# Attention's results and half of its queries turned by transposing transfers instead of TensorE

## The chip, the cores and the metric

The kernel runs on one core of one Trainium2 chip. The metric is the time of one execution on the device, in microseconds (us); of several executions the median is given.

A core has five engines with a queue of instructions each: TensorE (PE) multiplies matrices and writes to PSUM only; VectorE (DVE), ScalarE (ACT) and GpSimd (POOL) work on elements; SyncE (SP) here only issues transfers. Transfers (DMAs) are issued from SP's queue or POOL's and move data between main memory and SBUF, or within SBUF. Each queue works in its order, and an instruction that has to wait holds up those behind it.

## The reference, cut to what matters

Two layers in a row. The first is attention in which every block of 96 tokens looks at one block of mixed keys and values; the mixing matrix comes from five Sinkhorn steps:

```python
# B, H, S, D = 4, 8, 768, 64; 8 blocks of 96 tokens
k_sorted = einsum('bhij,bhjcd->bhicd', P, k_b)
v_sorted = einsum('bhij,bhjcd->bhicd', P, v_b)
scores = scale * matmul(q_b, k_sb.T)          # within a block: 96 x 96
attn = exp(scores - max) ; attn /= sum
attn_out = matmul(attn, v_sb)
x = attn_out.transpose(0, 2, 1, 3).reshape(B * S, H * D)   # 3072 x 512
```

The second is a mixture of eight experts, all of them applied to all 3072 tokens and weighted by a table P that comes from eight Sinkhorn steps over the logits of all tokens:

```python
logits = x @ w_gate                            # 512 x 8
for e in range(8):
    out += P[:, e:e+1] * (maximum(x @ w1[e], 0) @ w2[e])
```

The inputs are float32; the kernel multiplies in bfloat16 and accumulates in float32.

## The kernel before, in words

**Layout.** A batch's keys, values and queries come into SBUF (`load_batch`, L67, issued by POOL, which converts them to bfloat16) with the 768 tokens spread over 128 partitions, six tokens to a partition. A token is thus named by a partition c and a place kk from 0 to 5. The attention matmuls need the head's 64 channels on the partitions, and the expert layer needs x with its 512 channels on the partitions (`xtT`, four groups of 128 channels, one for each pair of heads). So queries are turned before they are used, and results after.

**Steps of attention.** For each batch bb and pair of heads hp there are five steps. Each has a letter in the plans, so "s2" is the scores of pair 2:

- "k", `keys` (L210): twelve matmuls with the mixing matrix that sort and turn the keys at once; VectorE copies them out of PSUM into `kTs`.
- "q", `queries` (L188): the queries are turned on TensorE. In batches 0 and 1 this takes twelve transposes of 64 channels; in batches 2 and 3 POOL first puts a pair's channels side by side (`qr`, L201) and six transposes of 128 channels follow (L205). ScalarE copies the result out of PSUM into `qTs`, and puts the tokens back into their order as it does so (L208).
- "s", `scores` (L231): sixteen matmuls of 96x96 (L239), and exponentials by ScalarE into `atp` (L247).
- "m", `mix` (L250): sixteen matmuls of the exponentials with the sorted values and a column of ones (L257); VectorE divides by the sums (L260, L261) into `og`, which has tokens on its partitions.
- "t", `turn` (L265): eight transposes on TensorE (L268), and a copy out of PSUM into `xtT` (L271).

The values are sorted by `sort_values` (L176): eight matmuls, copies by ScalarE into `vs`, and then `hop` (L169), which moves them within SBUF from the spread layout into blocks of 96 tokens (`vsb`) by eight transfers, one for each block: the even blocks are issued on SP, the odd ones on POOL (L172). A mix reads all eight. `logits` (L276) multiplies `xtT` by the gate's weights (L283).

**Order.** Batch 0 is attended to first, alone. From there to batch 3, attention is woven together with the expert layer's first expert over batches 0 and 1: `first_two` (L465) is a generator of 56 units of TensorE work, 28 for each batch. A hidden unit is four matmuls with w1 (L379) and an output unit four matmuls with w2 (L388). The strings of steps, such as `usual` (L500), are plans: a comma joins steps, and a blank marks a place where units may be put. `run_both` and `weave` (L451) say how many. The hidden units of batch 1 read batch 1's `xtT`, the first of them right after k0 of batch 2. TensorE keeps its written order, and so do the operations under `pin`; elsewhere a scheduler sets the order of an engine's queue and puts in the waits. `sum_x` (L139) is VectorE's preparation of `xtT` for the later experts.

After batch 3, `last_two` (L739) does the first expert for batches 2 and 3, `balance` (L554) the eight Sinkhorn steps, and the other seven experts follow in a scheme that takes seven products where eight would be usual (`hidden`, L595, and `output7`, L673). That part is some four fifths of the run.

## Time and profile before

| | |
|---|---|
| Median of three executions | 680.24 us (679.92 to 681.83) |
| The profiled execution | 679.37 us, of which the span from the first to the last instruction is 677.4 us |
| TensorE busy | 651.2 us, 96% of the span |
| VectorE, ScalarE, POOL busy | 541.6, 298.2, 473.5 us |
| Batch 0, up to its last turn | about the first 31 us |
| Attention of batches 1 to 3 with the first expert | about 31 to 113.5 us |
| First expert on batches 2 and 3, balance, second expert begun | 113.5 to 171 us |
| Experts 1 to 7 | to the end |

How to read it: a line of the timeline gives the start in us from the span's start, the length, the engine, the line of the kernel, what is written and read, and how many alike follow one another; a bracket at the end tells how long the engine was idle before it and what released it. Matmuls are pipelined: a group's length includes some 0.17 us until the last result is out, so the cost of a group on TensorE is read from its start to the start of the next one. For transfers the time from issue to landing is given. "SPq" is the time of an instruction on SP's queue.

### The profile page before, as it was taken

To read this page: it belongs to the slowest core of one execution; us is meant where nothing else is said; L and a number is where in the kernel's file an instruction comes from. 1 tells how busy PE (TensorE), PEld (TensorE's weight loads), DVE (VectorE), ACT (ScalarE), POOL (GpSimd) and SP (SyncE) were. 2 spreads that over 40 slices of the span, in tenths; PEclk is the share of its full clock that TensorE was granted. 3 is DMA by queue.
4 is the path that set the end of the run, shared out by engine and by line. 5 is a ranking of instruction groups with operands and counts; after the bars stand their busy time and mean duration, and the time that the engine had idled before them with its cause. 6 is when DMAs were issued, how large, how long until landed. Compare 5 with 4: busy or idle time off the path is not lost.

```text
span 677.4 us, 13154 instructions
## 1 busy us (share of the span) xinstructions
PE 651.2 (96%) x5043; PEld 434.7 (64%) x5122; DVE 541.6 (80%) x1131; ACT 298.2 (44%) x541; POOL 473.5 (70%) x499
## 2 busy tenths in 40 slices
PE   4899999999999999999999999999999999999996
PEld 2656766554666666666666666666666666666675
DVE  6617768663788889888888889888898888888896
ACT  4575763469533343434333343333433343333430
POOL 4542435007987988898997898689886999646745
PEclk9999999999999999999999999999999999999999
DMA  9898973101240340030303040034003120001223
GB/s 159 143 215 132 160 133 47 19 1 24 40 62 1 63 63 1 1 63 10 55 1 57 7 64 1 2 63 63 1 1 64 19 45 1 0 1 63 94 78 141
DMA packets 32415, 36.57 MB, mean 54 GB/s; under 512 B 2016, under 2 KB 25312, under 8 KB 32352
## 3 DMA queue, kind: packets, MB, share of 16 engines
q0 software_dynamic: 26912, 27.82, 25.9%
q1 hardware_dynamic: 5440, 7.90, 3.6%
q8 instruction: 40, 0.66, 0.4%
q14 instruction: 23, 0.19, 0.1%
HBM read 52.45 MB, written 6.29 MB: 87 GB/s over the span
## 4 chain that ended last, share of the span: by engine, by line
PE 72%; DVE 1%; issue 1%; POOL 1%; ACT 0%; DVEq 0%
PE oacc L688 37%; PE bk L601 34%; PE bk L688 1%; DVE osbl L653 1%; POOL hs L671 1%; DVE hT L637 0%; DVE hT L640 0%; ACT p L621 0%; DVEq L653 0%
## 5 line engine op out<-in xcount | busy, mean ns | idle before, releaser
L653 DVE SCALAR_TENSOR_TENSOR osbl<-oacc,glog,osbl 128x256 f32<-128x256 f32 (+1 forms) x490 | 255.6, 522 | 61.3 <-PE oacc L688 61.2
L671 POOL TENSOR_TENSOR hs<-hT 128x512 bf16<-128x512 bf16 (+2 forms) x105 | 99.5, 961 | 68.4 <-DVE hT L640 68.2
L601 PE MATMUL bk<-xtT,w1e 128*128 128x512 bf16 x475 | 143.5, 379 | 0.9
L688 PEld LDWEIGHTS <-hT 128*128 128x128 bf16 x1008 | 98.6, 98 | 64.5 <-issue 1.3
L688 PEld LDWEIGHTS <-hs 128*128 128x128 bf16 x1008 | 98.5, 98 | 64.6 <-POOL hs L671 1.5
L688 PE MATMUL oacc<-w2e,hT 128*128 128x256 bf16 x796 | 119.6, 273 | 1.0 <-ACT hT L643 0.5
L643 ACT ACTIVATE hT<-bk 128x512 bf16<-128x512 f32 x84 | 50.3, 599 | 158.7 <-PE bk L601 140.9
L671 POOL TENSOR_TENSOR hs<-hT,hs 128x512 bf16<-128x512 bf16 (+2 forms) x105 | 100.0, 959 | 4.9
L671 POOL TENSOR_TENSOR hs<-hs,hT 128x512 bf16<-128x512 bf16 (+2 forms) x105 | 99.9, 959 | 4.2 <-ACT hT L643 0.4
L601 PE MATMUL bk<-xc,wc 128*128 128x512 bf16 x319 | 96.2, 379 | 0.6 <-ACT p L621 0.2
L688 PE MATMUL oacc<-w2e,hs 128*128 128x256 bf16 x612 | 92.0, 273 | 1.6 <-POOL hs L671 0.9
L629 ACT COPY u<-bk 128x512 f32<-128x512 f32 x84 | 49.3, 587 | 95.2 <-PE bk L601 83.6
L601 PEld LDWEIGHTS <-w1e 128*128 128x128 bf16 x672 | 65.7, 98 | 10.5
L637 DVE CUSTOM_DVE_ANT_0 hT<-bk,p 128x512 bf16<-128x512 f32 x84 | 58.1, 692 | 11.8 <-ACT p L634 6.4
L647 DVE SCALAR_TENSOR_TENSOR h<-bk,hT 128x512 bf16<-128x512 f32 x84 | 57.2, 681 | 5.7 <-ACT hT L643 5.7
L634 ACT COPY p<-bk 128x512 f32<-128x512 f32 x84 | 49.4, 588 | 23.5 <-PE bk L601 23.5
L621 ACT COPY p<-bk 128x512 f32<-128x512 f32 x84 | 49.4, 588 | 20.1 <-PE bk L601 20.1
L625 DVE CUSTOM_DVE_ANT_0 hT<-bk,p 128x512 bf16<-128x512 f32 x84 | 57.2, 681 | 1.1 <-ACT hT L381 0.6
L640 DVE CUSTOM_DVE_ANT_0 hT<-bk,u 128x512 bf16<-128x512 f32 x84 | 57.2, 680 | 1.0 <-PE bk L601 1.0
L688 PE MATMUL oacc<-w2s,hs 128*128 128x256 bf16 x364 | 54.8, 273 | 0.3
L601 PEld LDWEIGHTS <-wc 128*128 128x128 bf16 x504 | 49.3, 98 | 8.0 <-issue 0.4
L601 PE MATMUL bk<-xtT,wc 128*128 128x512 bf16 x159 | 48.0, 379 | 0.0
(136 smaller groups left out, 827.9 us busy)
## 6 DMA issues: line engine op xcount, KB each, us to landing
w2e<-in_moe_w_dram POOLq DMA_DIRECT2D x8, 1024.0 KB, 8.8
w1e<-in_moe_w_dram POOLq DMA_DIRECT2D x7, 1024.0 KB, 8.3
out_dram<-osbl SPq DMA_DIRECT2D x23, 256.0 KB, 2.0
kvq<-in_v_dram POOLq DMA_DIRECT2D x3, 768.0 KB, 9.0
kvq<-in_k_dram POOLq DMA_DIRECT2D x3, 768.0 KB, 11.6
vsb<-vs SPq DMA_DIRECT2D x16, 97.5 KB, 4.5
vsb<-vs POOLq DMA_DIRECT2D x16, 97.5 KB, 4.0
kvq<-in_q_dram POOLq DMA_DIRECT2D x4, 384.0 KB, 9.6
```

The source lines that it names most:

```text
L601: hold(nc.tensor.matmul(ps, wa[:, kk, :], xa[:, kk, :], start=(first and kk == 0), stop=(kk == 1), skip_group_check=True))
L621: nc.scalar.copy(p1, u)
L625: nc.vector._custom_dve(TENSOR_ADD_SAT, out=c11, in0=w, in1=p1, s0=TOP, s1=0.0)
L629: nc.scalar.copy(u2, u)
L634: nc.scalar.copy(p5, v)
L637: nc.vector._custom_dve(TENSOR_ADD_SAT, out=c22, in0=u, in1=p5, s0=TOP, s1=0.0)
L640: nc.vector._custom_dve(TENSOR_ADD_SAT, out=c12, in0=v, in1=u2, s0=TOP, s1=0.0)
L643: nc.scalar.activation(out=c21, in_=u, func=AF.Relu)
L647: nc.vector.scalar_tensor_tensor(out=h3[e, p][:, i, :], in0=u, scalar=0.0, in1=c22, op0=ALU.max, op1=ALU.subtract)
L653: nc.vector.scalar_tensor_tensor(out=o, in0=ps, scalar=glog[:, t, e:e + 1], in1=o, op0=ALU.mult, op1=ALU.add)
L671: nc.gpsimd.tensor_tensor(out=c, in0=a, in1=b, op=o)
L688: nc.tensor.matmul(ps, h[:, fb, :], w[:, fb, :], start=(first and fb == 0), stop=(fb == 3), skip_group_check=True)
```

## The change

Three kinds of turns leave TensorE, and what they need is rearranged:

- **Results.** For batches 1 and 2, and for three of the four pairs of batch 3, `turn` issues one transposing transfer on SP that reads `og` (96 tokens by 1024) and writes the pair's part of `xtT` (128 channels by 768 tokens). Batch 0 and the last pair of batch 3 stay on TensorE.
- **Queries of batches 2 and 3.** A new function, `queries_across`, has POOL put all four pairs of a batch side by side (`qr`) and issues one transposing transfer for each on SP, from 128 partitions of 768 into `qTs`. It is called ahead of the batch's value sort. Batch 1's queries stay on TensorE.
- **The tokens' order.** The transfer leaves a batch's queries in the order kk, c where ScalarE's copy had made c, kk of it. The score matmuls of these batches therefore read six runs of 16 tokens, and the exponentials read PSUM across and write in the tokens' order.
- **Buffers.** `og` and `qr` have four buffers instead of two.
- **Plans.** All four query steps of batch 1 now come before its scores; mixes and turns stand together; batch 1's logits come after three places of batch 2, batch 2's after three places of batch 3, and batch 3's near the end; the units of the first expert are dealt out anew, 56 as before. Batch 2's value sort comes after m3 of batch 1 instead of before it.

In SP's queue the order around each seam becomes: the four turns of a batch, the four query transfers of the next batch, and that batch's four transfers of sorted values.

```diff
@@ queries
-        if bb < 2:
-            for kk in range(6):
-                for h in range(2):
-                    pin(nc.tensor.matmul(qps[64 * h:64 * h + 64, kk, :], ...
-        else:
-            qr = sp.tile([128, 6, 2, 64], BF16, name="qr", bufs=2)
-            nc.gpsimd.tensor_copy(
-                qr.rearrange("p kk h d -> p h kk d"),
-                qt[bb][:, 2 * hp:2 * hp + 2].rearrange("p h (kk d) -> p h kk d", d=64))
-            for kk in range(6):
-                pin(nc.tensor.matmul(qps[:, kk, :], qr[:, kk].rearrange("p h d -> p (h d)"),
+        for kk in range(6):
+            for h in range(2):
+                pin(nc.tensor.matmul(qps[64 * h:64 * h + 64, kk, :],
+                                     qt[bb][:, 2 * hp + h, kk * 64:kk * 64 + 64],
                                      Ibig, is_transpose=True, start=True, stop=True))
+    def queries_across(bb):
+        for hp in range(4):
+            qr = sp.tile([128, 6, 2, 64], BF16, name="qr", bufs=4)
+            pin(nc.gpsimd.tensor_copy(
+                qr.rearrange("p kk h d -> p h kk d"),
+                qt[bb][:, 2 * hp:2 * hp + 2].rearrange("p h (kk d) -> p h kk d", d=64)))
+            qT[bb, hp] = sp.tile([128, 6, 128], BF16, name="qTs", bufs=4)
+            pin(nc.sync.dma_start_transpose(
+                out=qT[bb, hp], in_=qr.rearrange("p kk h d -> p (kk h d)")))
@@ scores
-                        qT[bb, hp][r, 16 * i:16 * i + 16].rearrange("p c kk -> p (c kk)"),
+                        (qT[bb, hp][r, :, 16 * i:16 * i + 16] if bb > 1 else
+                         qT[bb, hp][r, 16 * i:16 * i + 16].rearrange("p c kk -> p (c kk)")),
...
+                if bb > 1:
+                    to = to.rearrange("p j (c kk) -> p j c kk", kk=6)
+                    of = of.rearrange("p j (kk c) -> p j c kk", kk=6)
+                nc.scalar.activation(out=to, in_=of, func=AF.Exp, scale=scale)
@@ mix
-            og[bb, hp] = sp.tile([128, NB, 2, 64], BF16, name="og", bufs=2)
+            og[bb, hp] = sp.tile([128, NB, 2, 64], BF16, name="og", bufs=4)
@@ turn
+        if 0 < bb < 3 or bb == 3 and hp < 3:
+            pin(nc.sync.dma_start_transpose(
+                out=xtT[:, hp, bb * S:(bb + 1) * S].rearrange("p (i c) -> p i c", i=NB),
+                in_=og[bb, hp][0:96].rearrange("p i h d -> p (i h d)")))
+            return
@@ the order
-        at1 = attention(1, bank1, "k0 k1 k2 q0 q1 s0 q2 s1 k3 q3 s2 "
-                                  "m0 s3 m1,t0 m2,t1 m3 t2 t3,l0 l3")
-        run_both(at1, (1, 1, 1, 1, 0, 1, 0, 1, 1, 0, 1))
+        at1 = attention(1, bank1, "k0 k1 k2 q0 q1 q2 q3 s0 s1 k3 s2 "
+                                  "m0,t0 s3 m1,t1 m2,t2 m3,t3")
+        run_both(at1, (1, 1, 1, 1, 0, 0, 0, 1, 1, 1, 1))
         load_batch(2, [(x, 0, 8) for x in "vkq"])
         build_r(2, nc.gpsimd, 4)
-        run_both(at1, (1, 1, 1, 1))
+        run_both(at1, (1, 1, 1, 1, 1))
+        queries_across(2)
         run_both(sort_values(2, bank1), (1, 0, 1, 0, 1))
-        run_both(at1, (1, 0, 0, 0))
-        usual = "q0,q1,k0 k1,s0,q2 k2,s1,q3 m0 k3,s2 m1,t0 s3 m2,t1 m3 t2 t3,l0 l3"
+        usual = "k0 k1,s0 k2,s1 m0,t0 k3,s2 m1,t1 s3 m2,t2 m3 t3"
...
+            weave(at1, ex, 3, 3)
+            logits(bb - 1, bank1, (0, 1, 2, 3))
+            weave(at1, ex, 2, 2)
+            if bb == 2:
+                load_batch(3, [(x, 0, 8) for x in "vkq"])
+                build_r(3, nc.gpsimd, 4)
+                weave(at1, ex, 5, 4)
+                queries_across(3)
+                weave(sort_values(3, bank1), ex, 5, 5)
             else:
...
+                weave(at1, ex, 2, 4)
+                logits(3, bank1, (0, 1, 2, 3))
```

More of the change, by code (lines that the diff above doesn't have):

```diff
@@ L191, in queries @@
             qps = bank([128, 6, 128], BF16)
-        if bb < 2:
-            for kk in range(6):
-                for h in range(2):
-                    pin(nc.tensor.matmul(qps[64 * h:64 * h + 64, kk, :],
-                                         qt[bb][:, 2 * hp + h, kk * 64:kk * 64 + 64],
-                                         Ibig, is_transpose=True, start=True, stop=True))
-        else:
-            qr = sp.tile([128, 6, 2, 64], BF16, name="qr", bufs=2)
-            nc.gpsimd.tensor_copy(
-                qr.rearrange("p kk h d -> p h kk d"),
-                qt[bb][:, 2 * hp:2 * hp + 2].rearrange("p h (kk d) -> p h kk d", d=64))
-            for kk in range(6):
-                pin(nc.tensor.matmul(qps[:, kk, :], qr[:, kk].rearrange("p h d -> p (h d)"),
+        for kk in range(6):
+            for h in range(2):
+                pin(nc.tensor.matmul(qps[64 * h:64 * h + 64, kk, :],
+                                     qt[bb][:, 2 * hp + h, kk * 64:kk * 64 + 64],
                                      Ibig, is_transpose=True, start=True, stop=True))
@@ L246, in scores @@
                     new_at(bb, hp, h)
-                nc.scalar.activation(out=at[bb, hp, h][0:96, 4 * b:4 * b + 4],
-                                     in_=sps[h][0:96], func=AF.Exp, scale=scale)
+                to, of = at[bb, hp, h][0:96, 4 * b:4 * b + 4], sps[h][0:96]
+                if bb > 1:
+                    to = to.rearrange("p j (c kk) -> p j c kk", kk=6)
+                    of = of.rearrange("p j (kk c) -> p j c kk", kk=6)
+                nc.scalar.activation(out=to, in_=of, func=AF.Exp, scale=scale)
     def mix(bb, hp, h, bank):
         if h == 0:
-            og[bb, hp] = sp.tile([128, NB, 2, 64], BF16, name="og", bufs=2)
+            og[bb, hp] = sp.tile([128, NB, 2, 64], BF16, name="og", bufs=4)
         for b in range(2):
@@ L334, in wide_mix @@
     def wide_mix(hp, pair, extra):
-        og[0, hp] = sp.tile([128, NB, 2, 64], BF16, name="og", bufs=2)
+        og[0, hp] = sp.tile([128, NB, 2, 64], BF16, name="og", bufs=4)
         for h in range(2):
@@ L363, in step @@
                 turn(bb, hp, bank, nc.vector.tensor_copy)
-            elif what == "l":
-                logits(bb, bank, (0, 1, 2) if hp == 0 else (3,))
             else:
@@ L491 @@
         run_both(sort_values(1, bank1), (1, 1, 1, 1, 0))
-        at1 = attention(1, bank1, "k0 k1 k2 q0 q1 s0 q2 s1 k3 q3 s2 "
-                                  "m0 s3 m1,t0 m2,t1 m3 t2 t3,l0 l3")
-        run_both(at1, (1, 1, 1, 1, 0, 1, 0, 1, 1, 0, 1))
+        at1 = attention(1, bank1, "k0 k1 k2 q0 q1 q2 q3 s0 s1 k3 s2 "
+                                  "m0,t0 s3 m1,t1 m2,t2 m3,t3")
+        run_both(at1, (1, 1, 1, 1, 0, 0, 0, 1, 1, 1, 1))
         load_batch(2, [(x, 0, 8) for x in "vkq"])
         build_r(2, nc.gpsimd, 4)
-        run_both(at1, (1, 1, 1, 1))
+        run_both(at1, (1, 1, 1, 1, 1))
+        queries_across(2)
         run_both(sort_values(2, bank1), (1, 0, 1, 0, 1))
-        run_both(at1, (1, 0, 0, 0))
-        usual = "q0,q1,k0 k1,s0,q2 k2,s1,q3 m0 k3,s2 m1,t0 s3 m2,t1 m3 t2 t3,l0 l3"
-        for bb, ns in ((2, (5, 3, 2, 4)), (3, (5, 4, 0, 5))):
+        usual = "k0 k1,s0 k2,s1 m0,t0 k3,s2 m1,t1 s3 m2,t2 m3 t3"
+        for bb in (2, 3):
             at1 = attention(bb, bank1, usual)
-            weave(at1, ex, 5, ns[0])
-            if bb + 1 < B:
-                load_batch(bb + 1, [(x, 0, 8) for x in "vkq"])
-                build_r(bb + 1, nc.gpsimd, 4)
+            weave(at1, ex, 3, 3)
[7 more added lines that the diff above has]
+                weave(sort_values(3, bank1), ex, 5, 5)
             else:
@@ L509 @@
                 sums = sum_w(1)
-            weave(at1, ex, 3, ns[1])
-            if bb + 1 < B:
-                weave(sort_values(bb + 1, bank1), ex, 5, ns[2])
-            else:
+                weave(at1, ex, 3, 4)
                 for _ in sums:
@@ L518 @@
                     next(x0)
-            weave(at1, ex, 4, ns[3])
-        for _ in ex:
-            pass
+                weave(at1, ex, 2, 4)
+                logits(3, bank1, (0, 1, 2, 3))
+                for _ in ex:
+                    pass
     actx.close()
```

## The prediction

> **What bounds the kernel now.** I read the busy shares first, then the windows by stage, then TensorE's order of work inside the stage that changes, and last the transfers. The page and the windows say that TensorE is the bound nearly everywhere:
>
> ```profile
> PE 651.2 (96%) x5043; PEld 434.7 (64%) x5122; DVE 541.6 (80%) x1131; ACT 298.2 (44%) x541; POOL 473.5 (70%) x499
> ...
> PE 72%; DVE 1%; issue 1%; POOL 1%; ACT 0%; DVEq 0%
> ```
>
> ```profile
> 66.00:114.00 48.00, 46.65 (x682) 32.68 (x685) 35.93 (x111) 28.27 (x64) 24.84 (x29) 1.00 0.65 107
> ```
>
> The second fence is the stage of batches 2 and 3 (columns: stretch, then busy time and count of PE, PEld, DVE, ACT, POOL, then clock, DMA share, GB/s). TensorE is busy 46.65 of 48 us, so work taken from it there shortens the run, unless a wait takes its place. The order of its work around the seam between batches 1 and 2, in the timeline (start, length, work):
>
> ```profile
> 65.46 0.88 PE L257 MATMUL bank<-vsb,atp 96*96 96x65 bf16 x16
> 66.39 0.81 PE L388 MATMUL bank<-w2e,hTs 128*128 128x512 bf16 x3
> 67.04 1.07 PE L268 MATMUL bank<-Ibig,og 96*128 96x96 bf16 x16
> ...
> 68.83 0.30 PE L283 MATMUL bank<-wg,xtT 128*128 128x8 bf16 x6 [0.43 <-DVE xtT L271]
> 69.29 0.30 PE L283 MATMUL bank<-wg,xtT 128*128 128x8 bf16 x6 [0.16 <-DVE xtT L271]
> 69.45 0.83 PE L205 MATMUL bank<-Ibig,qr 128*128 128x128 bf16 x12
> 70.21 0.53 PE L218 MATMUL bank<-R,kvq 128*64 128x128 bf16 x12
> ...
> 72.37 0.51 PE L205 MATMUL bank<-Ibig,qr 128*128 128x128 bf16 x6
> 72.72 0.81 PE L379 MATMUL bank<-xtT,w1e 128*128 128x384 bf16 x4
> ...
> 79.72 0.51 PE L268 MATMUL bank<-Ibig,og 96*128 96x96 bf16 x8
> 80.07 0.82 PE L379 MATMUL bank<-xtT,w1e 128*128 128x384 bf16 x4
> ```
>
> The reader is to take from it what a step costs from its start to the next start: a turn of results (L268) 0.35, a turn of one head pair's queries (L205) 0.35 to 0.38, a feed-forward unit 0.65 (L379) or 0.865 (L388), a key group (L218) 0.46, a mix (L257) 0.70, a score group (L239) 0.49. TensorE waits only where a brace stands. The transfers of the sorted values (L172, issued in three different places) show what SP's queue costs:
>
> ```profile
> L172 SPq DMA_DIRECT2D vsb<-vs x16: 571/624/1167, 17.6 to 90.0; - x16
> ...
> DMA to landing us min/median/max: 2.8/4.1/6.8
> ```
>
> One such transfer of 97.5 KB holds SP's queue 0.57 to 1.17 us and lands 2.8 to 6.8 us after its issue. Asked by window, those at 87 to 91 us took 2.9 to 3.7, those at 65 to 69 us 2.8 to 5.5, and those at 42 to 46 us, with weights and inputs in flight, 5.6 to 6.8.
>
> **What goes.** Eleven turns of results: 11 x 0.345 = 3.8 us of TensorE. Eight turns of queries: 0.76 + 0.35 + 0.33 for batch 2 and 0.76 + 0.35 + 0.34 for batch 3 = 2.9 us. The waits beside them go as well: 0.43 and 0.16 (logits on the copy of the turned results), 0.24 twice (a query turn on ScalarE's copy, at 74.72 and 97.41) = 1.07. Two query turns of batch 1 (q2, q3; 0.46 each) move ahead of the first use of the second weight, where TensorE now waits 1.17 us for a transfer: 0.92 of that is filled. Sum: -8.7 us. The copies out of PSUM that go with them (11 x 0.54 on VectorE, 8 x 0.8 on ScalarE) were off the path, for VectorE is busy 36 and ScalarE 28 of the 48 us; I count nothing for them.
>
> **What is added beside the path.** The exponentials of batches 2 and 3 read PSUM across (32 of 497 ns). The nearest row is ScalarE's own strided copy: 814 ns (L208) against 799 for a plain one (L271) of the same 768 columns, 2%, so 0.3 us on an engine with 20 us to spare: nothing. The score matmuls of these batches (128, pitch 31 ns) read their queries in six runs of 16 instead of one run of 96. No row shows TensorE reading so; from nothing to a doubled pitch, +4.0 us. I take nothing, as the runs are still contiguous, and keep the 4.0 for the range. The larger buffers cost nothing in time. On POOL the eight query copies stay (about 1.07 us each with VectorE busy beside it), but the four of batch 2 now stand in front of POOL's share of the sorted values, and batch 3's loads follow at once: from the landing of batch 2's queries at 62.7 us, 4 x 1.07 + 2.15 gives 69.2 us for those loads, against 72.2 now.
>
> **What is added on SP's queue.** Nineteen transposing transfers of 192 KB. Their price, X us of SP's queue each, is in no row. The nearest is the sorted-value transfer on the same queue. Ends: 0.62, if only the issue counts, and 2.9, if the queue is held until the data has landed. By bytes (1.97 times as many) the plain issue of 0.57 to 1.17 becomes 1.1 to 2.3; I take 1.8. Landing, from issue: 2.9 at least.
>
> What matters is what is queued behind them. In program order SP now does t3 of a batch, the four query turns of the next, and only then its four transfers of the sorted values, which mix 0 of that batch reads. Count both ways from the end of m3's matmuls.
>
> Batch 1 to 2. TensorE's way to m0: four output units (3.46), eight value sorts (1.30), three key groups (1.38), three hidden units (1.95), two score groups (0.98), logits (0.60) = 9.7, and 0.26 more to block 6, the last that SP brings. SP's way: VectorE finishes m3 1.36 us after TensorE (67.70 against 66.34 now), then t3 and four queries, 5 x 1.8 = 9.0, then 2.2 to the fourth issue (65.6 to 67.8 now), then the landing. Batch 3's loads are in flight by then (69.2 us on; the fourth issue stands near 73), so I take the slow end of the neighbouring window, 5.5, not 3.2. Total 18.1, against 9.9: a wait of 8.1 us, in pieces block by block. t3 itself is needed 5.2 us after m3 and lands at 4.3 to 7; q0 is needed at 6.3 and lands at 6.1 or later; both small waits lie inside the 8.1.
>
> Batch 2 to 3. TensorE has two more output units, so 11.4 + 0.26 = 11.7. SP: 1.36 + 9.0 + 2.2 + 3.2 = 15.8 (no load in flight). Wait: 4.1.
>
> The end of batch 3 keeps t3 on TensorE, and t0 to t2 have over 3 us before logits: nothing. From 172 us on the same program runs.
>
> Sum: -8.7 + 8.1 + 4.1 = +3.5 us. The profiled execution took 679.37 us (span 677.4 and 2.0 around it), 0.87 below the median of 680.24. So 682.9 against its own time, 683.7 as a median.
>
> **Where a page of notes bears on it.** The row first: 97.5 KB move between places in SBUF and land in 2.8 us at best. The Trainium skill, "VectorE: DVE Perf Modes", section "The three transpose paths", gives 1,309 ns for one 128x128 block of bf16 by transfer, against 390 on TensorE; by it six blocks in a row would take 7.9 us, and the sum would be that of the block rival below, whose number is worked out there from rows; no row here shows such a transfer. The other rule is a worry of a second kind. The first stage has 128x384 matmuls of 521 ns (L292), against 326 later (L179), though the granted clock reads 1.00 in both. The Trainium skill, "TensorE: Matmul & The Clock Gate", section on rules for kernel authors, says that a gap of over about 3 us brings half speed back; by it the wait of 8.1 us would cost some 2 us more. The trace shows both speeds, but no gap that long in mid-run.
>
> **The rivals.**
>
> *Cheap issue: faster.* If X is 0.62, SP's way for batch 2 is 1.36 + 3.1 + 2.2 + 3.2 to 5.5 = 9.9 to 12.2, a wait of 0 to 2.2. Batch 3 then waits on another chain: its queries land 14.4 us after an issue at 71 (85.4), POOL's four copies end at 89.2 or so, SP's values land at 95, and m0 is due at 89.5: 5.7, or 3.5 if batch 2 has waited. Sum -3.0: 677.2; down to 671.5 if this chain is quicker too. At X = 1.25 the sum is -8.7 + 5.4 + 1.3 = -2.0. The sign turns near X = 1.45. For it: SP has issued in 0.57. Against it: that was half the bytes, and unturned.
>
> *Even: within 0.3%.* X of 1.25 to 1.6, where the waits eat just what was saved: 678.5 to 682.
>
> *Block by block: much slower.* The transfer is worked off in blocks and the queue is held meanwhile; at X = 4 the waits are 19 and 15, TensorE also stands at t3 and q0 inside them, and the sum is +25.5: 705.7. For it: landing took up to 6.8 us for half the bytes. Against: those had eight transfers in flight.
>
> *Shared engines.* The turned transfers collide with batch 3's loads; a longer landing there alone moves the time by 2 to 3 us and is in the forecast.
>
> **How the numbers follow.** A measurement of this kernel tells 0.3% (2 us) from no change. Forecast (X from 1.6 to 2.9, 682 to 695): 0.42. Block by block: 0.09. Even: 0.13. Cheap issue: 0.36. So slower 0.51, same 0.13, faster 0.36. The range goes from 674.5 (cheap issue, half of its lower tail) to 695 (X = 2.9: waits of 13.6 and 9.6, +14), which takes in the 4.0 of the score matmuls at the forecast X. The forecast's own range is 682 to 695.
>
> **What would show it.** Transposing transfers on SP with 1.6 us or more from one issue to the next; TensorE's longest new waits at m0 of batches 2 and 3, released by the sorted-value transfers that SP issued (L172), not at t3's hidden unit or at s0; 136 fewer transposes on TensorE; nothing new after 172 us. Wrong if SP's sorted-value transfers are issued within 8 us of t3's issue, if the score matmuls' pitch rises, or if TensorE waits for POOL's query copies.

## The result: 3.4% slower, outside the range

The changed kernel takes 701.88 us (median of four executions, 700.95 to 710.87), the kernel before 680.74 us beside it: a ratio of 1.034, 95% interval 1.029 to 1.038. The forecast was 683.7 us with a range of 674.5 to 695.0. It had the side right, with a chance of 0.51, and the size wrong by 18 us.

The first profiled execution was the longest of the four, 710.87 us, 9 us above the others. I therefore had the same kernel run once more: 702.99 us in the median, and a profiled execution of 701.98 us with a span of 700.2. Unless it says otherwise, "after" below means this second profile. Line numbers are those of the changed kernel: mixes are L262, scores L240, logits L293, the transfers of the sorted values still L172, the queries' transfers L208, the results' L272.

TensorE's share on the page of the first profile, and its part in the chain that ended last, against 96% and 72% before:

```profile
PE 659.1 (93%) x4986; PEld 433.2 (61%) x4986; DVE 536.4 (76%) x1120; ACT 293.3 (41%) x533; POOL 471.7 (67%) x499
...
PE 69%; DVE 1%; POOL 1%; issue 0%; ACT 0%; DVEq 0%
```

The stage of batches 2 and 3 in the second profile (same columns as before):

```profile
66.00:114.00 48.00, 28.21 (x364) 17.89 (x360) 20.39 (x57) 17.65 (x43) 15.92 (x22) 0.83 1.01 160
```

5122 weight loads have become 4986: the 136 transposes are gone. But in the stage that they left, TensorE is now busy 28 of 48 us instead of 47 (364 matmuls fall into them instead of 682, since the stage lasts longer), and the granted clock is 0.83 on average, where it was 1.00. These are the places where it stands, in the timeline (start, length, work, and in the bracket the idle time before and its releaser):

```profile
80.96 0.37 PE L262 MATMUL bank<-vsb,atp 96*96 96x65 bf16 x2 [8.22 <-DMA vsb<-vs]
...
82.45 0.37 PE L262 MATMUL bank<-vsb,atp 96*96 96x65 bf16 x2 [0.50 <-DMA vsb<-vs]
...
111.54 0.37 PE L262 MATMUL bank<-vsb,atp 96*96 96x65 bf16 x2 [7.12 <-DMA vsb<-vs]
...
112.94 0.30 PE L262 MATMUL bank<-vsb,atp 96*96 96x65 bf16 x2 [1.02 <-DMA vsb<-vs]
...
114.34 1.17 PE L262 MATMUL bank<-vsb,atp 96*96 96x65 bf16 x12 [1.10 <-DMA vsb<-vs]
...
133.58 0.48 PE L293 MATMUL bank<-wg,xtT 128*128 128x8 bf16 x12 [4.92 <-DMA xtT<-og]
```

The first two belong to mix 0 of batch 2, the next three to mix 0 of batch 3, the last to batch 3's logits, which wait for the transfer t2. SP's queue in the same profile (start, time until the last of a group is issued):

```profile
66.25 7.78 SPq L208 DMA_TRANSPOSE qTs<-qr  x4
74.12 3.29 SPq L172 DMA_DIRECT2D vsb<-vs  x4
...
95.69 6.98 SPq L208 DMA_TRANSPOSE qTs<-qr  x4
102.77 3.88 SPq L172 DMA_DIRECT2D vsb<-vs  x4
```

So the sorted values stand behind the four query transfers, as forecast. And this is what one transfer costs (length in ns on the queue, least, median and most; then the time from issue to landing):

```profile
L208 SPq DMA_TRANSPOSE qTs<-qr x8: 1210/1228/3653, 66.2 to 99.7; - x8
...
DMA to landing us min/median/max: 2.7/3.9/10.8
```

The least is what matters first: 1.21 us on the queue (1.37 from one issue to the next) and 2.7 us to land, less than the 1.8 and 2.9 of the forecast. The most is what went wrong: the last of each four held the queue for 3.0 to 3.7 us and landed after 9.6 and 10.8. The results' transfers in the same view; the one that took 9.1 us to land is t2 of batch 3:

```profile
L272 SPq DMA_TRANSPOSE xtT<-og x11: 1212/1256/2279, 56.5 to 124.4; - x11
...
DMA to landing us min/median/max: 2.8/4.0/9.1
```

The granted clock behind the waits (second number from the start of the line: TensorE's busy us; third from the end: the clock):

```profile
77.00:81.00 4.00, 0.04 (x1) 0.04 (x2) 0.00 (x0) 0.00 (x0) 0.00 (x0) 0.51 1.24 208
81.00:84.00 3.00, 1.82 (x17) 1.57 (x18) 0.68 (x4) 0.00 (x0) 0.00 (x0) 0.50 1.29 223
84.00:87.00 3.00, 3.00 (x35) 1.77 (x33) 2.24 (x7) 0.74 (x2) 0.00 (x0) 0.50 1.31 203
...
114.00:118.00 4.00, 3.66 (x40) 2.52 (x42) 2.48 (x9) 0.49 (x1) 3.74 (x4) 0.50 0.02 5
...
133.00:136.00 3.00, 2.42 (x18) 1.15 (x19) 0.38 (x2) 0.00 (x0) 0.00 (x0) 0.50 0.00 0
```

It falls to a half while TensorE stands and stays there for 5 to 6.5 us after work goes on. The three stretches at half clock last 10.24, 10.24 and 6.83 us, which is three, three and two steps of 3.41 us; in every trace of this case the half-speed stretches behind waits last one such step or a whole number of them. What the slow clock takes is the busy time times what the clock lacks of 1: over all stretches 2.6 us behind mix 0 of batch 2, 2.2 behind that of batch 3, 2.5 behind the logits, 7.3 in all.

The account of the second profile against the span before (677.4), beside the terms of the forecast:

| | forecast, us | measured, us |
|---|---|---|
| taken from TensorE, with the waits beside it | -8.7 | -8.7, taken over from the forecast (136 loads fewer; the wait for the second weight 0.25 instead of 1.17); the other rows and the span leave -9.4 for it |
| mix 0 of batch 2 | +8.1 | +9.4 (8.22, 0.50, and 0.33 and 0.34) |
| small waits ahead of it | within the 8.1 | +1.4 (0.78 before s0, 0.34 and 0.29 for t2 and t3 of batch 1) |
| mix 0 of batch 3 | +4.1 | +9.2 (7.12, 1.02, 1.10) |
| logits of batch 3 | 0 | +4.9 |
| slow clock | in words, about 2, not in the sum | +7.3 |
| sum | +3.5 | +23.5, where the span is 22.8 longer |

### The profile page after: what moved, and what is told of

It reads as the page before. It is cut to its first block, busy times and chain, and to the rows that moved or that the text cites. A ratio compares the mean times of both kernels' runs of the same rounds, so it can differ in the third digit from the quotient of the medians.

```text
span 709.1 us, 12989 instructions
## 1 busy us (share of the span) xinstructions
PE 659.1 (93%) x4986; PEld 433.2 (61%) x4986; DVE 536.4 (76%) x1120; ACT 293.3 (41%) x533; POOL 471.7 (67%) x499
## 4 chain that ended last, share of the span: by engine, by line
PE 69%; DVE 1%; POOL 1%; issue 0%; ACT 0%; DVEq 0%
PE oacc L699 35%; PE bk L612 34%; PE bk L699 1%; DVE osbl L664 1%; POOL hs L682 1%; DVE hT L648 0%; DVE hT L651 0%; ACT p L632 0%; DVEq L664 0%
## 5 line engine op out<-in xcount | busy, mean ns | idle before, releaser
L612 PE MATMUL bk<-xtT,w1e 128*128 128x512 bf16 x504 | 149.9, 380 | 0.0
L612 PE MATMUL bk<-xc,wc 128*128 128x512 bf16 x336 | 100.1, 380 | 0.2 <-ACT p L632 0.2
L612 PE MATMUL bk<-xtT,wc 128*128 128x512 bf16 x168 | 50.0, 380 | 0.0
```

The costliest lines, as they stand in the source:

```text
L612: hold(nc.tensor.matmul(ps, wa[:, kk, :], xa[:, kk, :], start=(first and kk == 0), stop=(kk == 1), skip_group_check=True))
```

## The experiments

All runs are compared with the kernel before on the same chip (679.5 to 680.7 us). Two theories stood at the start. *A, collision*: a transposing transfer alone is cheap, but it and whatever POOL has in flight (sorted values, loads of inputs and weights) stretch each other. *B, the queue*: the sorted values come late because of the order on SP alone. The second run of the changed kernel was expected so:

> The changed kernel once more, for a second profile: its first profiled execution took 710.87 us, 9 us over the median of the others, with a wait of 1.92 us for the second weight at 49.9 us and half speed behind it. Expected if that wait is what the first had for itself: no wait over 1 us before 66 us, the waits at mix 0 of 8 to 12 us and 6 to 9 us and the one of about 4 us at the logits of batch 3 as before, and a span of 699 to 702. If the long execution was of the same course: the wait of about 1.9 us again and a span near 709.

It was the first case, 702.99 us (1.036, 1.032 to 1.041), with the course shown above. In the first profile, and in that of the run below with t2 on TensorE, TensorE waited 1.92 and 2.67 us for the second weight from 48 us on, ran at about half speed behind that, and two query transfers of batch 2 took over 14 us to land, where here one took 9.6. Why that weight came late there is open.

### Batch 2: the loads, the queue, or both

Three edits of the changed kernel. The first holds back the loads of batch 3 (and of the first weight) on POOL until the sorted values have landed:

```diff
+        def gate(bb):
+            pin(nc.gpsimd.tensor_copy(
+                held, mkap(vsbt[bb % 2], [[VW, 96], [520, 2]], off=6 * 520 + 519)))
...
+                gate(2)
                 load_batch(3, [(x, 0, 8) for x in "vkq"])
...
+                gate(3)
                 load_w1(1)
```

> The changed kernel, with POOL made to hold back the loads of batch 3 (and of the second half of the first weight) until that batch's sorted values have landed; SP's queue has the same transfers in the same order. Theory A: with nothing large in flight q0 to q3 hold SP 1.2 us each and land in 2.8 to 3.5, the sorted values land in 3 to 4; SP's way is 1.4 + 6.1 + 2.2 + 3.2 = 12.9 against 9.9 of TensorE, so mix 0 of batch 2 waits 2 to 4 us instead of 11.6, mix 0 of batch 3 0 to 2 instead of 8.5, and little slow clock follows; batch 3's loads start some 10 us later and may cost up to 5 at their first use: 682 to 690. Theory B: the order on SP is the same, so the waits at mix 0 stay at 8 to 12 and 6 to 8, and the later loads come on top: 700 to 708.

The second clears SP's queue instead:

```diff
-            eng = nc.gpsimd if i % 2 else nc.sync
+            eng = nc.gpsimd if i % 2 or bb > 1 else nc.sync
```

> The changed kernel, with all eight transfers of the sorted values of batches 2 and 3 issued on POOL, so that nothing stands behind the queries' transfers on SP; the loads of batch 3 follow them on POOL as before. Theory A: the loads still run beside the queries' transfers, so q2 and q3 of batch 2 hold SP 3 to 5 us and land after 9 to 15; the wait moves from mix 0 to scores 2 and 3 and is smaller, 3 to 7 us in batch 2 and 0 to 4 in batch 3, with some slow clock: 686 to 695. Theory B: with the queue free the sorted values land 4 to 6 us after issue, mix 0 of neither batch waits, and no wait takes its place: what is left is the 4.1 at the logits of batch 3 and its clock, 680 to 684.

The third leaves batch 3's loads out:

```diff
-                load_batch(3, [(x, 0, 8) for x in "vkq"])
+                vt[3], kt[3], qt[3] = vt[2], kt[2], qt[2]
```

> The changed kernel without the loads of batch 3 (three of 0.79 MB): batch 3 is computed from batch 2's values, keys and queries, so its part of the output is another. SP's queue has the same transfers in the same order. Theory A (the loads are the larger part of what stretches the transfers): q2 and q3 of batch 2 land after 5 to 7 us instead of 14.5, the sorted values behind them after 3 to 4 instead of 10.5, mix 0 of batch 2 waits 2 to 5 us instead of 11.6, batch 3 waits little, and the granted clock falls less: 682 to 688. Theory B (the order of SP's queue alone): mix 0 of batch 2 still waits 8 us or more, and the time is 695 to 702.

The first took 699.47 us (1.031, 1.028 to 1.034), the second 691.2 (1.017, 1.015 to 1.020), the third 699.93 (1.029, 1.026 to 1.032). The waits of TensorE where the loads are held back:

```profile
78.91 0.37 PE L262 MATMUL bank<-vsb,atp 96*96 96x65 bf16 x2 [4.83 <-DMA vsb<-vs]
...
104.75 0.88 PE L240 MATMUL bank<-qTs,kTs 64*96 64x96 bf16 x16 [5.26 <-DMA qTs<-qr]
...
114.74 0.62 PE L262 MATMUL bank<-vsb,atp 96*96 96x65 bf16 x4 [4.12 <-DMA vsb<-vs]
```

and where there are none:

```profile
76.68 0.37 PE L262 MATMUL bank<-vsb,atp 96*96 96x65 bf16 x2 [4.77 <-DMA vsb<-vs]
...
106.43 0.37 PE L262 MATMUL bank<-vsb,atp 96*96 96x65 bf16 x2 [6.58 <-DMA vsb<-vs]
...
107.88 0.29 PE L262 MATMUL bank<-vsb,atp 96*96 96x65 bf16 x2 [1.09 <-DMA vsb<-vs]
...
128.09 0.48 PE L293 MATMUL bank<-wg,xtT 128*128 128x8 bf16 x12 [4.78 <-DMA xtT<-og]
```

Both ways the first wait at mix 0 of batch 2 falls from 8.2 to 4.8 us: 3.4 of it are the loads. The other 4.8 need no load. With POOL's four transfers of sorted values in flight, the fourth query transfer still held the queue 2.67 us in the run without loads, and 3.56 us where they were held back, and SP's sorted values stood behind all four. What the loads add is in the landing: SP's sorted values of batch 2 landed after 3.2 to 4.3 us in these two runs, after 6.3 to 6.8 in the changed kernel. So neither theory has it alone. The wait fell as A had it, but both times lie where B had them (just under 700 to 708, and within 695 to 702), since batch 3 kept its own waits, which I had left out of A. Holding the loads back won little, 2 to 4 us: they then met the results' transfers of batch 2, batch 3's queries landed at 101 us, and s0 of batch 3 waited 5.3 us for its turned queries. The traffic was moved, not avoided. Clearing the queue won most, 11 us: the largest single wait left was 2.2 us. The time is in A's range (686 to 695), but the waits stood at the mixes and not, as A had it, at scores 2 and 3: the eight transfers on POOL and the query transfers were in flight together, POOL's last four of each batch landed after 5.8 to 7.9 us, mixes waited 10.0 us in eleven pieces, and the slow clock behind them took 7.9 us. The edit is not pure either: behind four more transfers on POOL, batch 3's loads were issued 2 to 4 us later.

### Batch 3: the weights' loads

The forecast took SP's sorted values of batch 3 to land after 3.2 us, "no load in flight". But POOL issues the load of a first weight (1 MB) at 100.7 us, right behind its own sorted values, and later that of a second weight at 123.3, beside t2. Two edits of the changed kernel, one for each:

```diff
+                gate(3)
                 load_w1(1)
```

> The changed kernel, with POOL made to hold back the load of the first weight in batch 3 until that batch's sorted values have landed; batch 3's own loads stay where they were. Theory G (this load, which the forecast took as not in flight, is what made the wait at mix 0 of batch 3 9.2 us instead of 4.1): SP's sorted values of batch 3 land 4 us after issue instead of 8.7, and the wait falls to 4 to 5.5; about 4 us faster than the changed kernel, 697 to 699, unless the later load is then waited for. Rival (the queue's order and POOL's own values make the wait): it stays at 8 us or more, 701 to 704.

```diff
-        if 0 < bb < 3 or bb == 3 and hp < 3:
+        if 0 < bb < 3 or bb == 3 and hp < 2:
...
-            at1 = attention(bb, bank1, usual)
+            at1 = attention(bb, bank1, usual if bb == 2 else usual.replace("m2,t2 m3", "m2 m3,t2"))
```

> The changed kernel, but t2 of batch 3 on TensorE, one unit after its mix; t0 and t1 stay transfers. Theory G (the wait of 4.9 us at batch 3's logits is t2's transfer, issued beside the load of a second weight and landing after 9 us): that wait and the 2.45 us of slow matmuls behind it go, 0.35 comes back: 7 us faster than the changed kernel, 695 to 696. Theory H (another thing is late there, t1's transfer or VectorE): a wait of 3 us or more stays at the logits, 699 or more.

With the first weight held: 694.6 us in the median of four that spread from 691.9 to 703.3 (ratio 1.020, 1.017 to 1.022), 7 to 8 us below the changed kernel where 4 were expected. SP's sorted values of batch 3 in that run, and then in the changed kernel (queue length in ns; issue to landing):

```profile
L172 SPq DMA_DIRECT2D vsb<-vs x4: 588/866/1606, 103.7 to 107.2; - x4
...
DMA to landing us min/median/max: 3.2/3.8/4.3
```

```profile
L172 SPq DMA_DIRECT2D vsb<-vs x4: 730/824/1360, 102.8 to 105.9; - x4
...
DMA to landing us min/median/max: 8.6/8.7/9.3
```

The wait at mix 0 of batch 3 was 3.24, 0.83 and 0.43 us, 4.5 in all, instead of 9.2: the load was the difference. The rest came from the logits, whose wait went too, since the second weight was now issued after t2 had landed; instead the balance waited 2.5 us for VectorE.

With t2 on TensorE: 697.54 us (1.030, 1.023 to 1.036), some 5 us below the changed kernel where 7 were expected. The logits waited for nothing and ran at clock 1.00. Its profile has the late second weight as well, so the rest can't be split further; the wait and its slow clock were t2's landing.

### The collision by itself

The kernel before, with four transfers that nothing of it needs:

```diff
         run_both(sort_values(2, bank1), (1, 0, 1, 0, 1))
+        for _ in range(4):
+            spare = sp.tile([128, 6, 128], BF16, name="spare", bufs=4)
+            pin(nc.sync.dma_start_transpose(out=spare, in_=xtT[:, 0, 0:S]))
```

> The kernel before, unchanged but for four spare transposing transfers of 192 KB on SP behind its sorted values of batch 2; nothing reads what they write, nothing is queued behind them until batch 3's sorted values some 20 us later. It measures the collision by itself. Theory A (the transfers and POOL's loads stretch each other): the first holds SP 1.2 us and lands in about 3, the ones issued while the loads of batch 3 are moving hold it 3 us or more and land after 7 to 15; the loads, which land 7.6, 11.4 and 14.4 us after issue without them, need 3 to 8 us more for the last, and TensorE meets that as a wait of 1 to 5 us before the queries of batch 3: 681 to 686. Theory B (only the queue's order): 1.2 us and 3 us for all four, loads as before: 679 to 681.

681.55 us (1.003, 1.000 to 1.006). The transfers were stretched as theory A has it, but "nothing waits" was not so: VectorE writes over these tokens later (`sum_x`) and waited 6.4 us until they had been read, so the time is not the collision's. Twice more, then, from a weight that stays, once turned and once plain:

```diff
+            pin(nc.sync.dma_start_transpose(out=spare, in_=w1t[0][:, 0, 0:S]))
```

> The spare transfers once more, read from the first expert's first weight, which nobody overwrites in this stage (in the run before VectorE had to wait 6.4 us with its in-place step on the tokens until they had been read, so that run's time was not the collision's). Four transposing transfers of 192 KB on SP behind the sorted values of batch 2. Theory A: again 2 to 4 us on the queue and 6 to 14 us to land for those beside the loads, and the last load of batch 3 lands 17 to 19 us after issue instead of 14.4; TensorE meets that as a wait of 1 to 4 us at the queries of batch 3, with slow clock if it is over 2: 681 to 685. Theory B: 1.2 and 3 us, loads as before, 679 to 680.5.

```diff
+            pin(nc.sync.dma_start(out=spare.rearrange("p a b -> p (a b)"), in_=w1t[0][:, 0, 0:S]))
```

> The same four transfers, of the same bytes, from and to the same places, but plain: the rows are copied, not turned. If the turning (or the small packets that come with it) is what stretches them and the loads: 0.6 to 1 us on the queue, 3 to 6 us to land, and the last load within 1 us of its 14.4: 679 to 680.5. If any 192 KB on SP beside the loads does it: landings of 6 to 14 us and the last load at 17 us or more, as with the turned ones.

Turned, 681.66 us (1.002, 1.001 to 1.004); plain, 679.52 (0.999, 0.998 to 1.001). The spare transfers in the view of their line, turned and then plain:

```profile
L501 SPq DMA_TRANSPOSE spare<-w1e x4: 1278/2235/4154, 68.7 to 74.6; - x4
...
DMA to landing us min/median/max: 5.8/8.7/14.2
```

```profile
L501 SPq DMA_DIRECT2D spare<-w1e x4: 593/923/1434, 68.7 to 72.1; - x4
...
DMA to landing us min/median/max: 4.2/4.8/6.1
```

And POOL's three loads of batch 3 (values, keys, queries) beside them, in the kernel before, beside the turned and beside the plain ones:

```profile
DMA to landing us min/median/max: 7.6/11.4/14.4
```

```profile
DMA to landing us min/median/max: 9.0/14.5/18.7
```

```profile
DMA to landing us min/median/max: 8.2/11.8/14.8
```

The same bytes between the same places: plain, they cost the last load 0.4 us; turned, 4.3 us, and themselves landed after 8.7 us in the median instead of 4.8. That is the collision, and it comes with the turning. Part of it is timing: the plain four had all been issued by 72.1 us, ahead of the first load, but the turned ones held the queue so long that the last two went out at 73.3 and 74.6 us, behind that load (72.3), and these are the ones that landed after 11.4 and 14.2 us. Nor does a plain transfer go free amid the loads: SP's sorted values in the changed kernel needed 6.3 to 6.8 us there. Behind the turned ones TensorE waited 1.72 us at the queries of batch 3 for POOL's copy, and the clock fell.

### Results alone

Queries back on TensorE, results by transfers:

```diff
-        queries_across(2)
-        usual = "k0 k1,s0 k2,s1 m0,t0 k3,s2 m1,t1 s3 m2,t2 m3 t3"
+        usual = "q0,q1,k0 k1,s0,q2 k2,s1,q3 m0,t0 k3,s2 m1,t1 s3 m2,t2 m3 t3"
...
-                queries_across(3)
```

> The results of batches 1 to 3 are turned by transfers as in the changed kernel; the queries of batches 2 and 3 are turned on TensorE again (q0 to q3 at their old places, scores and exponentials as before). Theory A (the transfers disturb each other: a turning transfer alone holds SP 1.2 us and lands in 2.8, and it is the loads of the next batch in flight beside the queries' transfers that stretch both; the waits that follow also bring the clock down): each result's transfer stays at 1.2 and 2.8, no wait over 1 us at mix 0 of batch 2 or 3, logits of batch 3 still wait 2 to 4 us for t2, which is issued beside the load of a second weight. Removed 3.8 + 0.6 of waits + 0.9, added about 4 and 2 of slow clock: 678 to 683. Theory B (only the order of SP's queue matters): t3 alone stands ahead of the sorted values, 1.2 us, which fits into the 1.8 us that they had to spare: no wait there, and nothing at batch 3's end from traffic: 675 to 677.

It took 694.38 us (1.022, 1.020 to 1.023), far from either number. POOL's timeline shows why:

```profile
65.12 3.59 POOL L200 COPY qr<-kvq 128x768 bf16<-128x768 bf16 x4 [15.14 <-DMA kvq<-in_q_dram]
68.66 0.94 POOL L72 DMA_DIRECT2D kvq<-in_v_dram  x1
...
73.36 2.15 POOL L172 DMA_DIRECT2D vsb<-vs  x4
```

I had left `qr` its four buffers. POOL then does all four copies and the loads before its sorted values, which landed 11 us after their issue, behind 2.4 MB. The fault was my edit's, and it shows the same thing from another side. With two buffers the order on POOL is that of the kernel before:

```diff
-            qr = sp.tile([128, 6, 2, 64], BF16, name="qr", bufs=4)
+            qr = sp.tile([128, 6, 2, 64], BF16, name="qr", bufs=2)
```

> Results alone by transfers as in the run before it, but with two buffers for the regrouped queries instead of four, which puts POOL's share of the sorted values ahead of batch 3's loads again, as in the kernel before (the earlier run had all four copies and the loads first, and those values landed 11 us after their issue). Theory E (the 14.7 us lost there come from POOL's values queued behind 2.4 MB of loads, not from the results' transfers): no wait at mix 0 of batch 2 above 2 us, full clock there: 674 to 679, faster than the kernel before by the 3.8 of the turns and part of the waits beside them. Theory F (the results' transfers themselves disturb the stage): mix 0 still waits over 5 us, and the time stays above 688.

679.71 us: 0.999, 0.997 to 1.001, just above theory E's range. No wait at mix 0, but no gain:

```profile
91.72 0.51 PE L204 MATMUL bank<-Ibig,qr 128*128 128x128 bf16 x6 [3.59 <-POOL qr L200]
...
93.50 1.46 PE L395 MATMUL bank<-xtT,w1e 128*128 128x384 bf16 x4
```

The four results of batch 2 go out at 76 to 85 us, amid batch 3's loads; the queries' load takes 17.5 us instead of 14.4, POOL's copy is late, TensorE waits 3.6 us, and then a hidden unit takes 1.46 us instead of 0.82. What eleven turns had saved is gone. So, the turns of batch 2 back on TensorE as well, one unit after their mix:

```diff
-        if 0 < bb < 3 or bb == 3 and hp < 3:
+        if bb == 1 or bb == 3 and hp < 3:
```

> Results of batches 1 and 3 (t0 to t2) by transfers, those of batch 2 on TensorE one unit after their mix, queries on TensorE: seven turns of results less on TensorE. In the run with batch 2's results by transfers too, its four were issued while batch 3's loads were moving, landed after 7 to 11 us, and the load of the queries needed 17.5 us instead of 14.4, for which TensorE waited 3.6 us and ran slow for another 2.2. Theory A (collision): without them the queries' load lands after about 14.4 again, that wait and the slow stretch go, four turns of 0.35 come back: 679.7 - 5.8 + 1.4 = 675 to 677, faster than the kernel before. Rival (the wait has to do with POOL's order or with batch 1's transfers): the wait stays at 2 to 4 us and the time at 679 to 681.

676.96 us: 0.996, interval 0.994 to 0.998, as theory A had it. That is 2.6 us faster than the kernel before, and the best of all. Its two halves of the stage:

```profile
66.00:90.00 24.00, 22.48 (x319) 15.09 (x316) 19.27 (x52) 16.25 (x36) 10.48 (x14) 1.00 0.83 136
90.00:114.00 24.00, 23.76 (x333) 15.98 (x332) 17.49 (x54) 14.19 (x32) 13.91 (x16) 1.00 0.62 105
```

TensorE is as busy as before, at clock 1.00; the three loads landed after 8.9, 11.8 and 14.8 us.

### Queries alone

```diff
-        if 0 < bb < 3 or bb == 3 and hp < 3:
+        if False:
```

> The queries of batches 2 and 3 are turned by transfers as in the changed kernel; all results are turned on TensorE again. Theory A: the queries' transfers still run beside batch 3's loads, so q2 and q3 of batch 2 still hold SP 3 to 5 us and land after 9 to 15; mix 0 of batch 2 waits 8 to 11 us and of batch 3 some 4 to 7, the clock falls behind each, no wait at the logits of batch 3: 694 to 700. Theory B: SP's queue is shorter by t3 alone (1.2 us), so the waits of 11.6 and 8.5 become 10.4 and 7.3, and 4.1 at the logits goes: 696 to 699. The two differ in the holds and landings alone; the run says which part carries the loss.

701.93 us (1.033, 1.032 to 1.035), above both ranges, again for a reason of my own: in this plan a turn stands right behind its mix, and on TensorE it waits there for VectorE, 12.6 us in eleven pieces. With the turns one unit later, as in the kernel before:

```diff
-                                  "m0,t0 s3 m1,t1 m2,t2 m3,t3")
+                                  "m0 s3 m1,t0 m2,t1 m3 t2 t3")
...
-        usual = "k0 k1,s0 k2,s1 m0,t0 k3,s2 m1,t1 s3 m2,t2 m3 t3"
+        run_both(at1, (0, 0))
+        usual = "k0 k1,s0 k2,s1 m0 k3,s2 m1,t0 s3 m2,t1 m3 t2 t3"
...
```

> Queries alone by transfers as in the earlier run, but with each result's turn on TensorE one unit after its mix, as in the kernel before (the earlier run had it right behind the mix, where TensorE waited 12.6 us in eleven pieces for VectorE). If those pieces were a fault of that run's order: they fall below 2 us in sum, and what is left is the queries' transfers: q0 and q1 quick, q2 and q3 stretched beside POOL's values and loads, mix 0 of batch 2 waiting 5 to 10 us, of batch 3 some 2 to 6, with slow clock behind: 688 to 697. If the queries' transfers cost nothing beyond the queue's 1.2 us each: 678 to 683.

688.86 us (1.010, 1.007 to 1.014), in the first case's range; the four executions spread from 685.17 to 695.54, and the profile is of the one of 685.17. The longest wait left:

```profile
78.08 0.37 PE L262 MATMUL bank<-vsb,atp 96*96 96x65 bf16 x2 [5.17 <-DMA vsb<-vs]
```

In batch 2 the fourth query transfer still went out beside POOL's sorted values and held the queue 2.10 us. In batch 3 all four held it 1.23 us, and mix 0 waited 0.57 us: with no results ahead of them the last went out at 94.4 us, 3.3 us before POOL's sorted values, where in the changed kernel it went out at 99.7, 1.2 us behind the first of them. Queries alone cost 9 us, results alone nothing, both together 21 to 23: the results' transfers push the queries' deeper into POOL's traffic.

### The clock

```diff
+                if bb > 1 and hp == 0:
+                    spare = bank([128, 512], F32)
+                    for _ in range(44 if bb == 2 else 30):
+                        pin(nc.tensor.matmul(spare, Ibig, xtT[:, 0, 0:512],
+                                             start=True, stop=True))
                 for h in range(2):
                     mix(bb, hp, h, bank)
```

> The changed kernel with spare matmuls (128x512, into a bank that is never read) ahead of mix 0: 44 in batch 2, 30 in batch 3, at full speed 9.4 and 6.4 us, about as long as TensorE stands still there. They add work and take nothing away. Theory C (the clock falls because TensorE stands still, and the half speed after the wait is a loss on top of it): the granted clock stays near 1.00 behind both places, the 3.8 and 3.1 us of slow matmuls behind them go, and the kernel is 5 to 7 us faster than the changed one: 694 to 697. Theory D (the slow stretches come with the traffic or are no loss of their own): the clock still drops there and the time is that of the changed kernel or above, 701 to 706.

703.01 us (1.033, 1.030 to 1.036), the time of the changed kernel. The test did not hold the clock up to the end:

```profile
78.00:80.00 2.00, 2.00 (x11) 0.88 (x9) 0.00 (x0) 0.00 (x0) 0.00 (x0) 1.00 1.27 190
...
82.00:84.00 2.00, 0.71 (x6) 0.46 (x7) 0.18 (x1) 0.00 (x0) 0.00 (x0) 1.00 1.27 230
84.00:86.00 2.00, 1.86 (x18) 0.96 (x19) 1.58 (x7) 0.03 (x1) 0.00 (x0) 0.67 1.32 205
86.00:88.00 2.00, 2.00 (x30) 1.47 (x29) 1.16 (x3) 1.17 (x3) 0.00 (x0) 0.50 1.31 204
```

While the spare matmuls ran, the clock stayed at 1.00 (78 to 80 us), with a DMA share of 1.27 and 190 GB/s. In the changed kernel TensorE stood at 77 to 81 us, and the clock was 0.51 beside a share of 1.24 and 208 GB/s. So the traffic alone does not bring the clock down; TensorE's standing still does, as theory C has it. But four short waits of 0.46 to 0.86 us behind the spare matmuls were enough to bring half speed.

By the same sum as above the slow stretches of this run take 5.9 us instead of 7.3. That does not show in the time, because the transfers came later here: the sorted values of batch 2 landed after 8.6 to 9.2 us instead of 6.3 to 6.8, those of batch 3 were issued 2.8 us later, and TensorE waited behind the spare matmuls all the same (2.3 and 3.05 us). So the run shows what brings the clock down, and not what it is worth to hold it up.

The other runs agree. With no wait over 1.2 us (the kernel before, and the best one) the clock is 1.00 from 40 to 140 us, with the same loads in flight; behind each wait of 1.7 to 12 us it fell, and a single one of these took 1.6 to 3.6 us, with little regard to its length (1.7 behind 1.92 and behind 3.59, 2.6 behind 8.22, 2.1 behind 11.4). The steps fit that: one step of 3.41 us at half speed, with TensorE busy throughout, takes 1.7 us. With shorter waits it went both ways: one of 1.49 us was followed by half speed (queries alone, first form) and one of 1.53 us was not (loads held back); the wait of 1.05 to 1.07 us near 31 us, which nearly all profiles have, was followed by half speed in two of them (loads held back, clearing the queue), which cost each 1.7 us, and by none in the others.

## Why the prediction was wrong

The forecast's sum was +3.5 us, the account's +23.5. Of the 20 us between them 7.3 are the slow clock, 5.1 mix 0 of batch 3, 4.9 the logits, and 2.7 the waits up to mix 0 of batch 2.

**What goes** fits: the 136 transposes are gone, and the rest of the account leaves -9.4 us for this term, forecast -8.7. One reading was a little short: the two turns in the line at 67.04 take 0.90 us, not 0.70.

**Beside the path** was right where it said nothing: a score group still takes 0.56 us and an exponential 498 ns (500 before), so the strided reads cost nothing that shows, and the 4.0 us kept for them were not needed. It was right that batch 3's loads move forward (71.0 us instead of 72.2), but this was not beside the path: they met SP's transfers.

**SP's queue.** The place was right: the longest new waits stand at mix 0 of batches 2 and 3, released by the sorted values that SP issued. The price X was wrong, and the wait nearly right by luck. Undisturbed, X is 1.37, not 1.8; with it the forecast's own sum would be -8.7 + 6.0 + 1.9 = -0.8, no change. But t3 was issued 1.4 us late, because VectorE finished m3 2.7 us after TensorE (63.6 against 60.9 us) and not 1.36; q0 followed it by 2.6 us instead of 1.37 (t3 held the queue 1.93 us, and q0's load landed at 65.3 us instead of 62.7, beside batch 1's results); the fourth query transfer was held 2.4 us longer; and the sorted values landed after 6.3 to 6.8 us instead of 5.5. The errors cancelled: 9.4 us at mix 0 of batch 2, 10.8 with the small waits ahead of it, forecast 8.1. The test "1.6 us or more from one issue to the next" failed for six of eight.

**Batch 2 to 3** is the first step that failed: "3.2 (no load in flight)". A load was in flight, the first weight's, and the landing took 8.7. With that load held back the wait was 4.5 us, close to the forecast's 4.1, again partly by luck: X was cheaper than forecast, and the fourth query transfer was held 3.48 us in that run. The profile before had the load, right behind POOL's last copy for batch 3:

```profile
94.32 0.80 POOL L82 DMA_DIRECT2D w1e<-in_moe_w_dram  x1
```

I had followed SP's queue and not asked what POOL issues next.

**The end of batch 3, "nothing"** is the second: t2 had 3 us of slack for a landing of 2.8, but landed after 9.1 beside the second weight's load. That was 4.9 us.

**The clock** is the third and largest: 7.3 us. I had it as a worry of about 2 us for one wait, outside the sum. The first stage should have warned me: its 128x384 matmuls took 521 ns, and in the half-speed stretches of the second profile such a matmul takes 524 to 527 ns, against 326 at full speed. The clock of 1.00 that I read beside the 521 was no measurement, for that trace's record of the clock begins at 18.5 us, behind those matmuls. The Trainium skill, "TensorE: Matmul & The Clock Gate", under "What's actually happening", has TensorE at half rate after an idle window of some 3.4 us that runs free, and until it has been busy for about as long. The trace agrees on the half (0.50) and on the step (3.41 us); but the clock fell behind single waits of 1.49, 1.72 and 1.92 us too, and behind four of less than 1 us, so here a gap need not reach 3.4 us to cost. By that page's figure I estimate 1.7 us for each wait, half of 3.4; the runs show 1.6 to 3.6. With it the forecast's two waits would have brought its sum to +6.9.

**The rivals.** *Cheap issue*, in its form with X = 1.25, had the price of the transfer nearly right, and the time wrong by over 20 us. *Block by block* had the size (705.7), but not its mechanism: the Trainium skill, "VectorE: DVE Perf Modes", "The three transpose paths", gives 1,309 ns for one 128x128 block; six blocks landed in 2.7 us, with no load in flight, so they are not worked off one after another at that price. *Shared engines* was the right one. I had given it 2 to 3 us, at one place, and counted it as part of the forecast; the runs put its part with the loads at 3.4 us at mix 0 of batch 2, 4.7 at that of batch 3 and 4.9 at the logits, before the clock.

What stays open: by what means a transposing transfer and a load hold each other up, and whether the clock's 7.3 us could have been kept with better filled waits.

## What to carry over

Price a transfer by what is in flight when it lands, not by its best row: list for each new transfer what the other queues issue in the 10 us around it, the weights that come next included. Each wait of more than 1.5 to 2 us that this change put into the matmul-bound stage cost 1.6 to 3.6 us of half speed on top of its length, so three short waits are dearer than one long one. Moving work from the bound engine to transfers paid where nobody waited for what they delay (here seven of nineteen, landing after 2.9 to 7.9 us, 0.4% faster) and turned into waits where they met loads.

## What the runs showed of the hardware that I had not expected

Undisturbed, a transposing transfer of 192 KB within SBUF lands as quickly as a plain one of half the size (2.7 to 2.9 us against 2.8 at best), whether 96 or 128 partitions are read; it holds the queue 1.21 us, the plain one 0.57. But it comes in small packets. The two transfer queues in the second profile (packets, MB, share of the DMA engines' span):

```profile
q0 software_dynamic: 26912, 27.82, 25.7%
q1 hardware_dynamic: 20640, 11.64, 7.1%
```

SP's queue had 5440 packets and 7.90 MB before. The nineteen transfers thus added 15,200 packets, 800 each, of some 246 bytes (3.74 MB by 15,200), where POOL's have 1,034 on average. In the two runs with spare transfers the bytes on SP's queue are the same, 8.69 MB, and the packets 8640 turned and 6016 plain: 800 and 144 for each transfer. The loads suffered beside the first and not beside the second. So the number of packets would be a cause that fits; no run changed it without the turning.

The stretching doesn't need much traffic: with four transfers of sorted values alone, 0.1 MB each, a query transfer was held 2.67 or 3.56 us and landed after 6.2 or 6.8 (the two runs without loads); with loads as well, 3.65 and 9.6. And a transposing transfer issued just behind a load can be as slow as the load: in four profiles t2 of batch 3 went out 1.1 to 2.6 us behind the second weight's load and landed 0.3 to 0.5 us after it (in the second profile at 133.53 us, the load at 133.21). And the order within one queue matters: on POOL, a transfer behind 2.4 MB of loads took 11 us to land, ahead of them 4.
